# Linear attention: half of relu(k) and a 32-bit copy of v on GpSimd, with re-ordered queues

## The chip, the cores and the metric

The kernel runs on one core of a Trainium2 chip. The metric is the device time of one execution in microseconds (us), the median of several runs. Engines: TensorE (PE, and PEld for its weight loads), VectorE (DVE), ScalarE (ACT), GpSimd (POOL), and SyncE (SP, which issues all DMA transfers here). Ratios below are the mean time of one kernel's fast runs over the mean time of the fast runs of the kernel before from the same rounds, so they are not quite the ratios of the medians that are quoted. "Before" was measured anew in every set of rounds: 200.88, 200.08, 200.99 and 200.26 us. e1 to e4, e5 to e8, and the second e5 with e9 to e11 ran on three different chips, so across these groups the ratios compare better than the medians.

## The reference

32 heads, 2048 positions, 128 features, bf16:

```python
phi_q = jnp.where(q > 0, q + 1, jnp.exp(q)) + 1e-6
phi_k = jnp.where(k > 0, k + 1, jnp.exp(k)) + 1e-6
kv = jnp.einsum("bhsd,bhse->bhde", phi_k, v)
z = jnp.einsum("bhsd->bhd", phi_k)
num = jnp.einsum("bhqd,bhde->bhqe", phi_q, kv)
den = jnp.einsum("bhqd,bhd->bhq", phi_q, z)[..., None] + 1e-6
return num / den
```

The kernels use phi(x) = (min(exp(x), 1) + 1e-6) + relu(x). The two terms are separate stationary operands of TensorE, which adds them up.

## The kernel before

A head has 16 tiles of 128 positions. Its steps, with the names used below:

| name | engine | work |
|---|---|---|
| ek, eq | ScalarE | exp(k), exp(q) of the whole head |
| em, emq | VectorE | min with 1 and add 1e-6, in SBUF |
| rk | VectorE | relu(k), SBUF to SBUF |
| rqa, rqb | ScalarE, VectorE | relu of the transposed q, read from PSUM, half each; in every fourth head ScalarE does all |
| v1 | GpSimd | copies v next to a column of ones |
| T | TensorE | 16 transposes of q |
| kv, then kvs | TensorE, then ScalarE | 32 matmuls; copy of the 128x129 sum |
| n | TensorE | numerator and denominator: 12 tiles (nA, later n.0), 4 tiles (nC, later n.1) |
| r, f | VectorE | reciprocal and multiply, read from PSUM |

```python
    NI = 8      # buffers for k, q, v
    NO = 6      # output buffers
    LAG = 2     # a store is issued two heads behind
# ...
        def emrk(h):
            s = h % 2
            add("DVE", f"em{h}", lambda e: e.tensor_scalar(
                em_sb[:, s], em_sb[:, s], 1.0, EPS, op0=ALU.min, op1=ALU.add), [f"ek{h}"])
            add("DVE", f"rk{h}", lambda e: e.tensor_scalar(
                rk_sb[:, s], k_sb[:, h % NI], 0.0, None, op0=ALU.max), [f"ldk{h}"] + ([f"kv{h - 2}"] if h >= 2 else []))
# ...
        def v1(h):
            dep = [f"ldv{h}"]
            if h >= 2:
                dep += [f"kv{h - 2}"]
            if h >= 3:
                dep += [f"nA{h - 3}"]        # the gate: not needed for the data
            add("POOL", f"v1{h}", lambda e: e.tensor_scalar(
                v1_sb[:, h % 2, :, 0:D], v_sb[:, h % NI].rearrange("p (j d) -> p j d", d=D), 1.0, 0.0,
                op0=ALU.mult, op1=ALU.add), dep)
# ... the order of the instructions, head i
            eq(i)
            rqa(i)
            kvs(i + 1)
            ek(i + 2)
            f(i - 1, "A")
            rqb(i)
            emq(i)
            f(i - 1, "C")
            emrk(i + 2)
            T(i + 1)
            nA(i)
            nC(i)
            kv(i + 2)
```

Of the kernel before, what the change touches and what calls it, by code (L numbers as in the profile page):

```python
# [8 lines left out]
ENGINES = ("PE", "DVE", "ACT", "POOL", "SP")  # L9

# [5 lines left out]
class Program:  # L16



    def __init__(self, sem):  # L20
        self.sem = sem
        self.ops = {e: [] for e in ENGINES}
        self.where = {}
        self.count = {}
        self.sems = {}

    def add(self, eng, key, fn, deps=(), dma=None, inc=True):

        name = dma if dma is not None else eng
        if dma is not None or inc:  # L30
            self.count[name] = self.count.get(name, 0) + (16 if dma is not None else 1)
        if key is not None:
            assert key not in self.where, key
            assert dma is not None or inc
            self.where[key] = (name, self.count[name], eng, len(self.ops[eng]))
        self.ops[eng].append((fn, tuple(deps), name, (16 if dma is not None else 1) if (dma is not None or inc) else 0))
# [47 lines left out]
def _eps_pieces():  # L84

    import struct

    def bf(x):
        u = struct.unpack("<I", struct.pack("<f", x))[0]
        u = (u + 0x7FFF + ((u >> 16) & 1)) & 0xFFFF0000  # L90
        return struct.unpack("<f", struct.pack("<I", u))[0]

    a = bf(EPS / 128)
    b = bf(EPS - 126 * a)
    return a, b, bf(EPS - 126 * a - b)


def bass_standalone__linear_attn_elu__prompt_kernel(nc: bass.Bass, q: bass.AP, k: bass.AP, v: bass.AP, out: bass.AP):
    B, H, S, D = q.shape
    assert D == P and S == 16 * P  # L100
    NT = S // P
    NH = B * H
    bf16, fp32 = mybir.dt.bfloat16, mybir.dt.float32
    N = NT * D
    NC = D + 1
    NI = 8
    NO = 6
    LAG = 2
# [4 lines left out]
    with ExitStack() as es:  # L113
# [11 lines left out]
        k_sb, q_sb, v_sb = sb([P, NI, N]), sb([P, NI, N]), sb([P, NI, N])  # L125
        em_sb, rk_sb = sb([P, 2, N]), sb([P, 2, N])
        v1_sb = sb([P, 2, NT, NC])
        emq_sb, rq_sb = sb([P, 2, N]), sb([P, 2, N])
        kvs_sb = sb([P, 2, NC])
        rden_sb = sb([P, 2, NT], fp32)  # L130
        o_sb = sb([P, NO, NT, D])
        ident, ones, epsr, one1 = sb([P, P]), sb([P, P]), sb([P, 3]), sb([P, 1])
        xT = alloc(nc.psum_tensor, [P, N], bf16)
# [3 lines left out]
        CO = 4 * 512  # L137

        def slot(t):
            if t < 12:  # L140
                return 512 * (t // 3) + NC * (t % 3)
            return CO + 512 * ((t - 12) // 2) + NC * ((t - 12) % 2)

        pr = Program(sem)
        add = pr.add


# [9 lines left out]
        for s in range(2):  # L157
            add("DVE", f"v1ones{s}", lambda g, s=s: g.memset(v1_sb[:, s, :, D:NC], 1.0))


        def load(name, dst, src, h, freed):
            dep = [f"{f}{h - NI}" for f in freed] if h >= NI else []
            add("SP", f"ld{name}{h}", lambda e: e.dma_start(
                dst[:, h % NI].rearrange("p (j d) -> p j d", d=D), rows(src, h)), dep, dma=f"{name}{h % NI}")

        def loads(h):
            load("k", k_sb, kf, h, ["ek", "rk"])
            load("q", q_sb, qf, h, ["T"])
            load("v", v_sb, vf, h, ["v1"])

        def store(h):
            s = h % NO
            if h < NH - 1:
                add("SP", f"st{h}", lambda e: e.dma_start(rows(of, h), o_sb[:, s]), [f"fA{h}", f"fC{h}"], dma=f"o{s}")
            else:
                add("SP", None, lambda e: e.dma_start(rows(of, h)[:, 0:12, :], o_sb[:, s, 0:12]), [f"fA{h}"], dma=f"o{s}")
                add("SP", f"st{h}", lambda e: e.dma_start(rows(of, h)[:, 12:NT, :], o_sb[:, s, 12:NT]), [f"fC{h}"],
                    dma=f"o{s}")

        for h in range(min(NI, NH)):  # L180
            loads(h)
        for h in range(NH + LAG):
            if h + NI < NH:
                loads(h + NI)
            if h >= LAG:
                store(h - LAG)


        def ek(h):
            add("ACT", f"ek{h}", lambda e: e.activation(em_sb[:, h % 2], k_sb[:, h % NI], ACT.Exp),  # L190
                [f"ldk{h}"] + ([f"kv{h - 2}"] if h >= 2 else []))

        def eq(h):
            add("ACT", f"eq{h}", lambda e: e.activation(emq_sb[:, h % 2], xT[:, :], ACT.Exp),  # L194
                [f"T{h}"] + ([f"nC{h - 2}"] if h >= 2 else []))

        def split(h):
            return h % 4 != 3

        def rqa(h):  # L200
            n = N // 2 if split(h) else N
            add("ACT", f"rqa{h}", lambda e: e.activation(rq_sb[:, h % 2, 0:n], xT[:, 0:n], ACT.Relu),  # L202
                [f"T{h}"] + ([f"nC{h - 2}"] if h >= 2 else []))

        def rqb(h):
            if split(h):
                add("DVE", f"rqb{h}", lambda e: e.tensor_scalar(  # L207
                    rq_sb[:, h % 2, N // 2:], xT[:, N // 2:], 0.0, None, op0=ALU.max),
                    [f"eq{h}"] + ([f"nC{h - 2}"] if h >= 2 else []))

        def rqs(h):
            return [f"rqa{h}"] + ([f"rqb{h}"] if split(h) else [])

        def kvs(h):
            add("ACT", f"kvs{h}", lambda e: e.activation(kvs_sb[:, h % 2], kv_ps, ACT.Copy),  # L215
                [f"kv{h}"] + ([f"nC{h - 2}"] if h >= 2 else []))

        def emrk(h):
            s = h % 2
            add("DVE", f"em{h}", lambda e: e.tensor_scalar(  # L220
                em_sb[:, s], em_sb[:, s], 1.0, EPS, op0=ALU.min, op1=ALU.add), [f"ek{h}"])
            add("DVE", f"rk{h}", lambda e: e.tensor_scalar(  # L222
                rk_sb[:, s], k_sb[:, h % NI], 0.0, None, op0=ALU.max), [f"ldk{h}"] + ([f"kv{h - 2}"] if h >= 2 else []))

        def emq(h):
            s = h % 2
            add("DVE", f"emq{h}", lambda e: e.tensor_scalar(  # L227
                emq_sb[:, s], emq_sb[:, s], 1.0, EPS, op0=ALU.min, op1=ALU.add), [f"eq{h}"])

        def v1(h):  # L230
            dep = [f"ldv{h}"]
            if h >= 2:
                dep += [f"kv{h - 2}"]
            if h >= 3:
                dep += [f"nA{h - 3}"]
            add("POOL", f"v1{h}", lambda e: e.tensor_scalar(  # L236
                v1_sb[:, h % 2, :, 0:D], v_sb[:, h % NI].rearrange("p (j d) -> p j d", d=D), 1.0, 0.0,
                op0=ALU.mult, op1=ALU.add), dep)

        def T(h):  # L240
            def f(e):
                for j in range(NT):
                    ins = e.transpose(xT[:, j * P:(j + 1) * P], q_sb[:, h % NI, j * D:(j + 1) * D], ident[:])  # L243
                return ins
            add("PE", f"T{h}", f, [f"ldq{h}", "ident"] + (([f"eq{h - 1}"] + rqs(h - 1)) if h else []))

        def kv(h):
            def f(e):
                for j in range(NT):
                    for part, src in ((0, em_sb), (1, rk_sb)):  # L250
                        ins = e.matmul(kv_ps, lhsT=src[:, h % 2, j * D:(j + 1) * D], rhs=v1_sb[:, h % 2, j, :],  # L251
                                       start=(j + part == 0), stop=(j == NT - 1 and part == 1))
                return ins
            add("PE", f"kv{h}", f, [f"em{h}", f"rk{h}", f"v1{h}", "v1ones0", "v1ones1"] + ([f"kvs{h - 1}"] if h else [])
                + ([f"fC{h - 3}"] if h >= 3 else []))

        def num(h, tiles, bank, n, e):
            s = h % 2
            e.matmul(_ap(o_ps[:, :], slot(tiles[0]) + D, [[NC, n]]), lhsT=ones[:], rhs=epsr[:, 0:n], start=True, stop=False,  # L259
                     skip_group_check=True)  # L260
            for t in tiles:
                o = o_ps[:, slot(t):slot(t) + NC]
                e.matmul(o, lhsT=emq_sb[:, s, t * P:(t + 1) * P], rhs=kvs_sb[:, s, :], start=False, stop=False,  # L263
                         skip_group_check=True)
                ins = e.matmul(o, lhsT=rq_sb[:, s, t * P:(t + 1) * P], rhs=kvs_sb[:, s, :], start=False, stop=True,  # L265
                               skip_group_check=True)
            return ins

        def nA(h):
            def f(e):  # L270
                for b in range(4):
                    ins = num(h, range(3 * b, 3 * b + 3), b, 3, e)
                return ins
# [3 lines left out]
        def nC(h):  # L277
            def f(e):
                num(h, (12, 13), 4, 2, e)
                return num(h, (14, 15), 5, 2, e)  # L280
# [126 lines left out]
```

## Time and profile before

200.87 us (199.35 to 201.48, three runs). The page of the profiled execution gives busy time and share of each engine (first lines), the DMA engines' busy tenths and GB/s in 40 slices of the span, and the chain that ended last by engine:

```profile
span 197.3 us, 6384 instructions
PE 170.6 (86%) x2842; PEld 160.5 (81%) x2842; DVE 161.6 (82%) x254; ACT 160.0 (81%) x129; POOL 68.4 (35%) x38
...
DMA  6999999999999999999999999999999622222133
GB/s 228 346 418 411 412 404 407 410 404 416 416 411 422 412 416 419 411 420 414 414 420 413 419 418 414 419 414 417 416 415 394 246 116 110 106 106 105 61 130 137
...
ACT 37%; PE 33%; DVE 22%; DMA 3%; issue 2%; POOL 1%; SPq 0%
```

No engine is full: three stand at 81 to 86%, and the chain alternates between them. DMA is at its rate (394 to 422 GB/s a slice) from 10 to about 155 us. The view of waits shows whom the engines waited for (total us, times, longest):

```profile
POOL la L236 <- PE la L265: 97.5, 29, 3.5
DVE la L220 <- ACT la L190: 27.4, 32, 7.1
ACT la L215 <- PE la L251: 23.0, 25, 4.0
...
POOL la L236 <- DMA la<-in_v_dram: 11.5, 3, 6.5
```

ScalarE's copy of kv (L215) waits for kv, and VectorE's em (L220) for exp(k). That is a chain through three engines: kv, kvs, ek, em, rk, next kv. GpSimd's wait is its gate and costs next to nothing: TensorE waited 0.2 us in all for the copy (same view). The timeline of one head on VectorE and GpSimd (start us, duration us, engine, line, operation; in brackets the idle time before):

```profile
103.40 0.69 DVE L220 TENSOR_SCALAR la<-la 128x2048 bf16<-128x2048 bf16 x1 [0.88 <-ACT la L190]
104.01 0.69 DVE L222 TENSOR_SCALAR la<-la 128x2048 bf16<-128x2048 bf16 x1
104.06 2.39 POOL L236 TENSOR_SCALAR la<-la 128x2048 bf16<-128x2048 bf16 x1 [3.13 <-PE la L265]
104.61 0.23 DVE L293 RECIPROCAL la<-la 128x12 f32<-128x12 f32 x1
...
104.87 1.76 DVE L299 TENSOR_TENSOR la<-la 128x1536 bf16<-128x1536 f32 x1
106.54 0.68 DVE L207 TENSOR_SCALAR la<-la 128x1024 bf16<-128x1024 bf16 x1
...
108.92 0.69 DVE L220 TENSOR_SCALAR la<-la 128x2048 bf16<-128x2048 bf16 x1 [0.28 <-ACT la L190]
```

The pitch of an operation is the distance from its start to the next start; it is shorter than the duration, because the next operation starts before the end (em ends at 104.09, rk starts at 104.01). From em to em a head takes 5.52 us. GpSimd's copy, 1.90 us where it is undisturbed, shows 2.39 us here: it started while VectorE's rk (L222) was under way.

### The profile page before, as it was taken

What the parts mean: (1) busy time and instruction counts of PE and PEld (TensorE: products, weight loads), DVE (VectorE), ACT (ScalarE), POOL (GpSimd) and SP (SyncE); (2) the same over time, 40 slices, a digit from 0 to 9 for tenths busy, and PEclk for the clock granted to TensorE, in tenths of its full rate; (3) what the DMA queues carried; (4) which work ended last, traced back from release to release, by engine and by line L of the source; (5) the groups of instructions that cost most, each with busy time, mean ns of one, the idle gap of its engine ahead of it and who ended that gap; (6) DMA issues with size and microseconds to landing.
All of it is one profiled execution on the core that took longest, in us unless ns stands there. A gap on an engine that the chain in (4) does not pass through costs nothing.

```text
span 197.3 us, 6384 instructions
## 1 busy us (share of the span) xinstructions
PE 170.6 (86%) x2842; PEld 160.5 (81%) x2842; DVE 161.6 (82%) x254; ACT 160.0 (81%) x129; POOL 68.4 (35%) x38
## 2 busy tenths in 40 slices
PE   6948999988898899988898889988898889988850
PEld 6938889888897889888897889888897889988850
DVE  0213899899989999899989999899989999899774
ACT  4563789988898889988898889988898889998530
POOL 1333343322344444332344444432344444431000
PEclk9997999999999999999999999999999999999985
DMA  6999999999999999999999999999999622222133
GB/s 228 346 418 411 412 404 407 410 404 416 416 411 422 412 416 419 411 420 414 414 420 413 419 418 414 419 414 417 416 415 394 246 116 110 106 106 105 61 130 137
DMA packets 18603, 67.52 MB, mean 342 GB/s; under 512 B 2064, under 2 KB 2192, under 8 KB 18576
## 3 DMA queue, kind: packets, MB, share of 16 engines
q1 hardware_dynamic: 18576, 67.12, 84.4%
q8 instruction: 22, 0.36, 0.7%
q14 instruction: 5, 0.04, 0.1%
HBM read 50.33 MB, written 16.78 MB: 340 GB/s over the span
## 4 chain that ended last, share of the span: by engine, by line
ACT 37%; PE 33%; DVE 22%; DMA 3%; issue 2%; POOL 1%; SPq 0%
ACT la L190 21%; PE la L251 18%; DVE la L299 9%; ACT la L202 6%; ACT la L194 6%; DVE la L220 6%; PE la L243 5%; PE la L263 5%; PE la L265 5%; DVE la L222 4%; DMA la<-in_v_dram 3%; ACT la L215 3%; DVE la L207 2%; DVE la L293 1%; POOL la L236 1%
## 5 line engine op out<-in xcount | busy, mean ns | idle before, releaser
L236 POOL TENSOR_SCALAR la<-la 128x2048 bf16<-128x2048 bf16 x32 | 67.7, 2116 | 109.1 <-PE la L265 97.5
L299 DVE TENSOR_TENSOR la<-la 128x1536 bf16<-128x1536 f32 x64 | 78.4, 1224 | 2.2
L251 PE MATMUL la<-la 128*128 128x129 bf16 x1024 | 65.3, 222 | 5.7 <-DVE la L222 5.4
L251 PEld LDWEIGHTS la<-la 128*128 128x128 bf16 x1024 | 59.7, 98 | 10.2 <-DVE la L222 7.1
L265 PE MATMUL la<-la 128*128 128x129 bf16 x512 | 66.7, 221 | 0.0
L263 PE MATMUL la<-la 128*128 128x129 bf16 x512 | 66.6, 220 | 0.0
L194 ACT ACTIVATE la<-la 128x2048 bf16<-128x2048 bf16 x32 | 59.8, 1869 | 3.7 <-PE la L243 3.7
L190 ACT ACTIVATE la<-la 128x2048 bf16<-128x2048 bf16 x32 | 60.9, 1902 | 1.9 <-DMA la<-in_k_dram 1.9
L265 PEld LDWEIGHTS la<-la 128*128 128x128 bf16 x512 | 49.8, 97 | 0.0
L263 PEld LDWEIGHTS la<-la 128*128 128x128 bf16 x512 | 47.6, 98 | 0.0
L243 PE MATMUL la<-la 128*128 128x128 bf16 x512 | 35.0, 222 | 12.7 <-DVE la L207 11.5
L220 DVE TENSOR_SCALAR la<-la 128x2048 bf16<-128x2048 bf16 x32 | 22.2, 694 | 27.4 <-ACT la L190 27.4
L243 PEld LDWEIGHTS la<-la 128*128 128x128 bf16 x512 | 29.6, 99 | 18.0 <-DVE la L207 15.5
L202 ACT ACTIVATE la<-la 128x1024 bf16<-128x1024 bf16 (+1 forms) x32 | 39.6, 1238 | 0.0
L259 PE MATMUL la<-la 128*128 128x3 bf16 (+1 forms) x192 | 32.5, 169 | 2.2 <-DVE la L227 2.2
L215 ACT ACTIVATE la<-la 128x129 bf16<-128x129 f32 x32 | 9.0, 280 | 23.0 <-PE la L251 23.0
L222 DVE TENSOR_SCALAR la<-la 128x2048 bf16<-128x2048 bf16 x32 | 22.0, 687 | 0.0
L227 DVE TENSOR_SCALAR la<-la 128x2048 bf16<-128x2048 bf16 x32 | 21.8, 683 | 0.0
L259 PEld LDWEIGHTS la<-la 128*128 128x128 bf16 x192 | 19.0, 99 | 2.4 <-DVE la L227 2.4
L207 DVE TENSOR_SCALAR la<-la 128x1024 bf16<-128x1024 bf16 x24 | 16.3, 681 | 0.0
L293 DVE RECIPROCAL la<-la 128x12 f32<-128x12 f32 x64 | 12.9, 201 | 2.5 <-PE la L265 2.5
L308 PE MATMUL la<-la 128*128 128x120 bf16 x90 | 7.6, 268 | 1.5 <-POOL la L149 1.5
(13 smaller groups left out, 9.9 us busy)
## 6 DMA issues: line engine op xcount, KB each, us to landing
la<-in_k_dram SPq DMA_DIRECT2D x32, 512.0 KB, 15.0
la<-in_q_dram SPq DMA_DIRECT2D x32, 512.0 KB, 15.0
la<-in_v_dram SPq DMA_DIRECT2D x32, 512.0 KB, 15.2
out_dram<-la SPq DMA_DIRECT2D x31, 512.0 KB, 15.1
out_dram<-la SPq DMA_DIRECT2D x1, 384.0 KB, 2.3
out_dram<-la SPq DMA_DIRECT2D x1, 128.0 KB, 2.1
```

Source lines behind the costliest of these rows:

```text
L190: add("ACT", f"ek{h}", lambda e: e.activation(em_sb[:, h % 2], k_sb[:, h % NI], ACT.Exp), [f"ldk{h}"] + ([f"kv{h - 2}"] if h >= 2 else []))
L194: add("ACT", f"eq{h}", lambda e: e.activation(emq_sb[:, h % 2], xT[:, :], ACT.Exp), [f"T{h}"] + ([f"nC{h - 2}"] if h >= 2 else []))
L202: add("ACT", f"rqa{h}", lambda e: e.activation(rq_sb[:, h % 2, 0:n], xT[:, 0:n], ACT.Relu), [f"T{h}"] + ([f"nC{h - 2}"] if h >= 2 else []))
L220: add("DVE", f"em{h}", lambda e: e.tensor_scalar(em_sb[:, s], em_sb[:, s], 1.0, EPS, op0=ALU.min, op1=ALU.add), [f"ek{h}"])
L222: add("DVE", f"rk{h}", lambda e: e.tensor_scalar(rk_sb[:, s], k_sb[:, h % NI], 0.0, None, op0=ALU.max), [f"ldk{h}"] + ([f"kv{h - 2}"] if h ...
L236: add("POOL", f"v1{h}", lambda e: e.tensor_scalar(v1_sb[:, h % 2, :, 0:D], v_sb[:, h % NI].rearrange("p (j d) -> p j d", d=D), 1.0, 0.0, o ...
L243: ins = e.transpose(xT[:, j * P:(j + 1) * P], q_sb[:, h % NI, j * D:(j + 1) * D], ident[:])
L251: ins = e.matmul(kv_ps, lhsT=src[:, h % 2, j * D:(j + 1) * D], rhs=v1_sb[:, h % 2, j, :], start=(j + part == 0), stop=(j == NT - 1 and par ...
L259: e.matmul(_ap(o_ps[:, :], slot(tiles[0]) + D, [[NC, n]]), lhsT=ones[:], rhs=epsr[:, 0:n], start=True, stop=False, skip_group_check=True)
L263: e.matmul(o, lhsT=emq_sb[:, s, t * P:(t + 1) * P], rhs=kvs_sb[:, s, :], start=False, stop=False, skip_group_check=True)
L265: ins = e.matmul(o, lhsT=rq_sb[:, s, t * P:(t + 1) * P], rhs=kvs_sb[:, s, :], start=False, stop=True, skip_group_check=True)
L299: add("DVE", f"f{which}{h}", lambda e: e.tensor_tensor(out=_ap(o_sb[:, :, :, :], ob + t0 * D, [[n * D, nb], [D, n], [1, D]]), in0=_ap(o_ps ...
```

## The change

Intent: take work from VectorE, lengthen the look-ahead between the engines, and let loads go ahead of stores. The new kernel names every instruction and gives each engine an explicit list (called "annealed" below). Its core:

```diff
-    NI = 8
-    NO = 6
+NI, NO, NE, NR, NV, NQ, NK = 7, 12, 2, 2, 2, 2, 2
+RKP = (8, 8, ...)   # tiles of relu(k) on GpSimd, of 16
+NA = (8, 8, ...)    # tiles of relu(q) on ScalarE, now 8 in every head
+def gate(name, h):
+    return []
 # relu(k), lower 8 tiles
 add("DVE", f"rkd{h}.{i}", ... e.tensor_scalar(rk_sb[...a:b], k_sb[...a:b], 0.0, None, op0=ALU.max)
 # relu(k), upper 8 tiles
+add("POOL", f"rkp{h}.{i}", ... e.tensor_scalar(rk_sb[...a:b], k_sb[...a:b], BIG, 0.0, op0=ALU.min, op1=ALU.max),
+    ldk + kv{h-2} + gate("rkp", h))
 # copy of v
-add("POOL", f"v1{h}", ... e.tensor_scalar(v1_sb[..., 0:D], v_sb[...], 1.0, 0.0, op0=ALU.mult, op1=ALU.add), dep)
+add("POOL", f"v1{h}.{i}", ... e.tensor_copy(v1_sb[...].bitcast(i32), v_sb[...].bitcast(i32)),
+    ldv + kv{h-2} + gate("v1", h))
 # orders, here around the 9th head (excerpts)
+"PE":  ... n8.0 T10.0 n8.1 kv10.0 kv10.1 n9.0 T11.0 n9.1 kv11.0 kv11.1 ...
+"DVE": ... r7.0 rkd10.0 f7.0 em10.0 r7.1 rqb9 f7.1 rkd11.0 r8.0 emq9.0 f8.0 em11.0 rqb10 r8.1 f8.1 ...
+"ACT": ... ek10.0 eq9.0 kvs9 rqa9 ek11.0 eq10.0 kvs10 rqa10 ...
+"POOL": ... rkp11.0 v111.0 v112.0 rkp13.0 v113.0 rkp12.0 rkp14.0 v114.0 ...
+"SP":  ... st4.0 ldq17.0 ldv15.0 st1.0 ldq21.0 ldv17.0 ldv18.0 st2.0 st3.0 ldk18.0 ldk20.0 ...
```

(The lists are cut; "..." also stands for indices.) Transposes and exp(q) now run two heads ahead of the division. The first head is done in halves, the last head's division and store in three groups.

## The prediction

> **What bounds the kernel now.** After a prologue, every head takes 5.525 us (pitch of exp(k) in the timeline). No engine is full in it. By pitches in the timeline: VectorE needs 5.25 us in the three heads of four in which it does half of relu(q), ScalarE 4.7 (5.5 in the fourth), TensorE about 4.7 (n 1.5 + 0.5, T 0.9, kv 1.8). The chain of waits alternates ScalarE (37%), TensorE (33%), VectorE (22%): kv -> kv copy -> exp(k) -> min/add. ScalarE waits 23.0 us in all for kv (waits view). GpSimd works 2.1 us per head, gated by the division matmuls so that it falls under VectorE's PSUM work. DMA runs at 416 GB/s up to 155 us but only early loads are waited for; 67.1 MB at 416 GB/s is 161 us, a floor close by. The first division matmul starts at 19.6 us, the last head's at 189.9, 7.4 us before the end.
>
> **What changes.** (a) Half of relu(k) leaves VectorE: 0.60 us of pitch -> about 0.33. (b) relu(q) is always split: ScalarE 4.7 us in every head; VectorE loses the cheap fourth head. Its sum: 0.26+0.60+1.68+0.60+0.33+0.21+0.60+0.69 = 4.97 us. (c) GpSimd gets two operations of 1024 elements; from 1.90 us for 2048 (undisturbed, timeline) I estimate 1.0 us each if a 32-bit element costs what a 16-bit one does: 2.0 us per head, as before. (d) The orders run transposes and exp(q) two heads ahead of the division, so the chain kv -> copy -> exp(k) -> kv is no longer closed within a head. (e) Twelve output buffers let stores wait.
>
> Sums now: VectorE 4.97, ScalarE 4.7, TensorE 4.7, DMA 2.1 MB / 416 GB/s = 5.04 us per head.
>
> **The cost.** The gate on GpSimd is gone: it starts when kv ends, by my count about half a microsecond before the large PSUM division ends, and min/add of exp(k) follows that at once. The Trainium skill, "SBUF — State Buffer", section "Who interferes with whom", says a VectorE operation in a two-port mode and a GpSimd operation block each other fully. This trace shows one side: GpSimd's copy takes 2.39 us instead of 1.90 when it starts 0.05 us into VectorE's relu(k) of 0.6 us. VectorE was never the blocked side here (each form varies by under 10 ns). I expect VectorE to lose 0.2 to 0.5 us per head.
>
> Period: about 5.2 us (4.97 without collisions, 5.6 with two per head). All of it is on the path.
>
> **Ends.** Halves and orders: first division matmul near 13 to 14 us, third near 25 us (30.7 before): about 5 us saved. Last head: about 6 us instead of 7.4.
>
> Span: 25.2 + 29 x 5.2 + 6 = 182; timed runs lie 2 to 4 us above the profiled span: about 184.5 us, range 178 to 194. Faster 0.90, same 0.06, slower 0.04.
>
> **Right or wrong in the profile.** Pitch of exp(k) 5.1 to 5.3 us; VectorE busy over 90% in the middle; GpSimd's two forms near 1.0 us each, many longer; VectorE's SBUF-to-SBUF forms now with a spread of several tenths; DMA near 1.0 almost to the end and less of a tail at 106 GB/s.
>
> **What would make it wrong.** The 32-bit copy or min-max costing twice per element (kv then waits for GpSimd); VectorE blocked twice per head; a load stuck behind another in the shuffled queue, seen as waits for DMA; the lower granted clock.

## The result

185.22 us (184.55 to 186.80, four runs): ratio 0.9238, 95% interval 0.9165 to 0.9310. The output is correct. The profiled execution is the slowest of the four (186.80 us), and the one before was a fast one: in all listed runs the time lies about 1.8 us above the span, so 197.3 us stands for about 199.1 us (an estimate). The two profiles therefore show 12.3 us of the 15.7 between the medians. The page of the changed kernel, the same parts as before:

```profile
span 185.0 us, 6438 instructions
PE 165.2 (89%) x2842; PEld 159.1 (86%) x2842; DVE 164.4 (89%) x266; ACT 155.2 (84%) x131; POOL 75.4 (41%) x71
...
DMA  5999999999999999938999999799999999968994
GB/s 175 322 411 416 407 409 405 409 406 375 352 318 423 408 410 415 403 109 272 414 417 378 302 416 414 283 363 391 348 414 418 413 424 412 384 251 335 398 409 170
...
DVE 38%; DMA 26%; PE 12%; SPq 10%; issue 6%; ACT 3%; POOL 2%; DVEq 0%; POOLq 0%
```

VectorE is busy longer than before (164.4 against 161.6 us) although it was given less to do (half of relu(k) less in every head, half of relu(q) more in every fourth). DMA has holes: 109 GB/s in the slice from 79 to 83 us. A quarter of the chain is now DMA. The waits:

```profile
POOL la L324 <- DMA la<-in_v_dram: 27.5, 13, 5.5
...
ACT la L345 <- PE la L368: 11.0, 14, 1.7
...
DVE la L316 <- DMA la<-in_k_dram: 4.7, 4, 2.4
...
DVE la L313 <- ACT la L310: 3.9, 4, 1.7
...
ACT la L336 <- PE la L331: 2.7, 4, 1.3
```

The chain through three engines is open: VectorE's wait for exp(k) fell from 27.4 to 3.9 us, ScalarE's for kv from 23.0 to 2.7. In its place stand 13 waits of GpSimd for v, 4 of VectorE for k, and a new one: ScalarE's exp(q) (L345) waits 11.0 us for the division's matmuls.

One head on VectorE without any GpSimd operation inside it (timeline):

```profile
101.48 0.22 DVE L375 RECIPROCAL la<-la 128x12 f32<-128x12 f32 x1
101.62 0.63 DVE L347 TENSOR_SCALAR la<-la 128x2048 bf16<-128x2048 bf16 x1
102.17 1.74 DVE L382 TENSOR_TENSOR la<-la 128x1536 bf16<-128x1536 f32 x1
103.83 0.68 DVE L313 TENSOR_SCALAR la<-la 128x2048 bf16<-128x2048 bf16 x1
104.47 0.43 DVE L316 TENSOR_SCALAR la<-la 128x1024 bf16<-128x1024 bf16 x1
104.82 0.18 DVE L375 RECIPROCAL la<-la 128x4 f32<-128x4 f32 x1
104.91 0.66 DVE L354 TENSOR_SCALAR la<-la 128x1024 bf16<-128x1024 bf16 x1
105.49 0.68 DVE L382 TENSOR_TENSOR la<-la 128x512 bf16<-128x512 f32 x1
106.08 0.22 DVE L375 RECIPROCAL la<-la 128x12 f32<-128x12 f32 x1
```

That is 4.60 us of VectorE work. Where GpSimd is at work it looks different (timeline, with GpSimd):

```profile
49.16 1.03 POOL L324 COPY la<-la 128x1024 int32<-128x1024 int32 x1
...
49.64 1.10 DVE L347 TENSOR_SCALAR la<-la 128x2048 bf16<-128x2048 bf16 x1
...
54.19 1.03 POOL L324 COPY la<-la 128x1024 int32<-128x1024 int32 x1
54.53 1.24 DVE L347 TENSOR_SCALAR la<-la 128x2048 bf16<-128x2048 bf16 x1
```

The same emq (L347) took 0.63 us in the quiet head; it takes 1.10 and 1.24 us when it starts 0.48 and 0.34 us into GpSimd's copy. Both times it ends 0.55 us after the copy does (50.19 and 55.22), so the earlier it starts, the longer it stands. rqb (L354), which reads PSUM, does not spread: it lies between 0.652 and 0.692 us in the whole trace. This is the side of the exclusion that the trace before could not show, and it agrees with the Trainium skill, "SBUF — State Buffer", section "Who interferes with whom", by which the later of the two waits until the earlier is through.

The holes in DMA come from the issuing queue (timeline of SP, with one line of TensorE, the transposes of head 14):

```profile
69.12 0.47 SPq L298 DMA_DIRECT2D la<-in_v_dram  x1
69.63 0.44 SPq L390 DMA_DIRECT2D out_dram<-la  x1
...
79.86 1.06 PE L342 MATMUL la<-la 128*128 128x128 bf16 x16
...
80.95 0.33 SPq L298 DMA_DIRECT2D la<-in_q_dram  x1
81.32 1.29 SPq L298 DMA_DIRECT2D la<-in_v_dram  x2
```

For 11 us nothing was issued. The next entry was the q load of head 21, whose buffer is freed by the transposes of head 14 (through at 80.92). Loads and stores behind it stood, whether they were ready or not.

Where the 12.3 us between the two profiled spans lie, from the first division matmul of a head:

| part | before | after | gain |
|---|---|---|---|
| start to head 2 | 30.84 | 26.73 | 4.1 |
| head 2 to head 31 | 159.02 (29 x 5.48) | 149.94 (29 x 5.17) | 9.1 |
| head 31 to end | 7.4 | 8.3 | -0.9 |

### The profile page after: what moved, and what is told of

It is laid out like the page before. It is cut to its first block, busy times and chain, and to the rows that moved or that the text cites. A ratio compares the mean times of both kernels' runs of the same rounds, so it can differ in the third digit from the quotient of the medians.

```text
span 185.0 us, 6438 instructions
## 1 busy us (share of the span) xinstructions
PE 165.2 (89%) x2842; PEld 159.1 (86%) x2842; DVE 164.4 (89%) x266; ACT 155.2 (84%) x131; POOL 75.4 (41%) x71
## 4 chain that ended last, share of the span: by engine, by line
DVE 38%; DMA 26%; PE 12%; SPq 10%; issue 6%; ACT 3%; POOL 2%; DVEq 0%; POOLq 0%
DVE la L382 18%; DMA la<-in_k_dram 11%; DMA out_dram<-la 9%; SPq L298 8%; DMA la<-in_v_dram 6%; DVE la L347 6%; DVE la L354 5%; DVE la L316 4%; DVE la L313 4%; PE la L366 4%; PE la L368 3%; PE la L342 3%; ACT la L345 2%; DVE la L375 2%; PE la L331 2%
## 5 line engine op out<-in xcount | busy, mean ns | idle before, releaser
L382 DVE TENSOR_TENSOR la<-la 128x1536 bf16<-128x1536 f32 (+2 forms) x65 | 77.5, 1196 | 1.2 <-DMA out_dram<-la 0.6
L345 ACT ACTIVATE la<-la 128x2048 bf16<-128x2048 bf16 (+1 forms) x33 | 60.2, 1825 | 12.3 <-PE la L368 11.0
L368 PE MATMUL la<-la 128*128 128x129 bf16 x512 | 69.6, 222 | 0.0
L366 PE MATMUL la<-la 128*128 128x129 bf16 x512 | 69.5, 221 | 0.0
L331 PE MATMUL la<-la 128*128 128x129 bf16 x1024 | 64.5, 219 | 2.1 <-POOL la L324 2.0
L310 ACT ACTIVATE la<-la 128x2048 bf16<-128x2048 bf16 (+1 forms) x33 | 61.3, 1860 | 3.0 <-DMA la<-in_k_dram 2.9
L320 POOL TENSOR_SCALAR la<-la 128x1024 bf16<-128x1024 bf16 x32 | 40.4, 1264 | 46.0 <-PE la L331 38.1
L324 POOL COPY la<-la 128x1024 int32<-128x1024 int32 (+1 forms) x33 | 35.2, 1070 | 44.3 <-DMA la<-in_v_dram 27.5
L342 PE MATMUL la<-la 128*128 128x128 bf16 x512 | 34.1, 219 | 5.3 <-DVE la L354 5.3
L351 ACT ACTIVATE la<-la 128x1024 bf16<-128x1024 bf16 x32 | 32.6, 1018 | 0.0
L313 DVE TENSOR_SCALAR la<-la 128x2048 bf16<-128x2048 bf16 (+1 forms) x33 | 24.5, 743 | 3.9 <-ACT la L310 3.9
L347 DVE TENSOR_SCALAR la<-la 128x2048 bf16<-128x2048 bf16 (+1 forms) x33 | 25.2, 765 | 1.8 <-ACT la L345 1.8
L316 DVE TENSOR_SCALAR la<-la 128x1024 bf16<-128x1024 bf16 x32 | 19.7, 615 | 5.5 <-DMA la<-in_k_dram 4.7
L354 DVE TENSOR_SCALAR la<-la 128x1024 bf16<-128x1024 bf16 x32 | 21.3, 667 | 0.5 <-ACT la L345 0.4
L375 DVE RECIPROCAL la<-la 128x12 f32<-128x12 f32 (+2 forms) x65 | 12.7, 197 | 3.7 <-PE la L368 3.0
```

The lines of the kernel that those rows point to most:

```text
L310: add("ACT", f"ek{h}.{i}", lambda e, a=a, b=b: e.activation(em_sb[:, h % NE, a:b], k_sb[:, h % NI, a:b], ACT.Exp), [f"ldk{h}.{i}"] + freed ...
L320: add("POOL", f"rkp{h}.{i}", lambda e, a=a, b=b: e.tensor_scalar(rk_sb[:, h % NR, a:b], k_sb[:, h % NI, a:b], BIG, 0.0, op0=ALU.min, op1=A ...
L324: add("POOL", f"v1{h}.{i}", lambda e, a=a, b=b: e.tensor_copy(v1_sb[:, h % NV, a:b, 0:D].bitcast(i32), v_sb[:, h % NI, a:b].bitcast(i32)), ...
L331: ins = e.matmul(kv_ps, lhsT=src[:, j], rhs=v1_sb[:, h % NV, j, 0:NC], start=(j + part == 0), stop=(j == NT - 1 and part == 1))
L342: ins = e.transpose(xT[:, j], q_sb[:, h % NI, j], ident[:])
L345: add("ACT", f"eq{h}.{i}", lambda e, a=a, b=b: e.activation(emq_sb[:, h % NQ, a:b], xT[:, a:b], ACT.Exp), [f"T{h}.{i}"] + freed(NQ, h, ("n ...
```

## The experiments

Theory A is the prediction's: VectorE, with its collisions with GpSimd, sets the pitch. Rival B: late loads from the order of the DMA queue set it, and collisions hide behind them. Twelve runs of eleven kernels were made on these and on what came up; all were correct. "Pitch" is the mean distance between the copies of kv of heads 3 and 29 on ScalarE (before 5.52, after 5.25).

### e1: relu(k) back on VectorE

```diff
-RKP = (8, 8, ...)
+RKP = (0,) * 32      # all of rk is rkd on VectorE; rkp dropped from GpSimd's list
```

> The changed kernel with all of relu(k) back on VectorE; GpSimd only copies v as 32-bit words. Theory A (VectorE, with its collisions with GpSimd, sets the pitch): VectorE gains 0.27 us of work a head, from 4.60 (the pitch of an undisturbed head at 101.5 to 106.1 us) to 4.87, and loses the collisions with one of GpSimd's two operations (about half of the 0.4 us that a head takes over 4.60 where no load is late). Net 0 to +0.15 us a head: 185 to 190 us. If moving relu(k) pays in full, it is 8 us slower: 193. Theory B (late loads set the pitch): no change, 185 within 1%, because the loads wait for the same events.

185.05 us, ratio 0.9256 (0.9160 to 0.9352); pitch 5.23. No difference from the changed kernel: the headline of the change pays nothing in its own setting. Both theories allowed for this, A by an even trade of work for collisions.

### e2: only the DMA queue mended

```diff
+    first = ORDER["SP"].split()
+    out = first[:first.index("ldk9.0")] + ["ldv6.0", "ldq6.0"]      # the first loads as they were
+    for h in range(7, 32):
+        out += [f"ldv{h}.0", f"ldk{h}.0", f"ldq{h}.0"]
+        if h >= 16:
+            out.append(f"st{h - 16}.0")
+    # the remaining stores follow in order (shortened: names put in as numbers)
```

> The changed kernel with only the order of the DMA queue replaced from the 20th load on: v, k, q of one head after another, a store seven heads behind. Theory A (VectorE with collisions sets the pitch): at most 1% faster, pitch stays near 5.25. Theory B (the queue stands behind loads that are asked for too early, 11 to 13 us at a time at 69.6, 105.7 and 147.9 us, and the next k and v come late): the waits of VectorE and GpSimd for k and v go (4.7 and 27.5 us now), DMA has no slice under 300 GB/s up to 140 us, the pitch falls from 5.25 to the 5.03 of the stretch from 37 to 58 us: 178 to 180 us.

180.86 us, ratio 0.9064 (0.8998 to 0.9129); pitch 5.05. The page's DMA line has no hole left:

```profile
GB/s 185 284 413 416 409 411 405 411 405 411 403 409 406 404 410 409 415 416 414 420 411 416 420 414 420 411 417 417 414 419 415 414 420 414 415 334 178 121 155 199
```

GpSimd's waits for v fell from 27.5 to 10.4 us. So B holds for 2.3% of the time by the medians (180.86 against 185.22), 1.9% by the ratios, a little less than expected. Heads of 5.5 to 5.8 us remain between heads of 4.72.

### e3 and e4: GpSimd tied to VectorE

```diff
 def gate(name, h):
-    return []
+    if h < 4:
+        return []
+    return [f"rkd{h}.0"] if name == "rkp" else [f"emq{h - 2}.0"]
```

with GpSimd's list made regular (rkp4 v14 rkp5 v15 ...). e3 does this alone, e4 with e2's queue.

> The changed kernel with GpSimd's two operations tied to VectorE: relu(k) starts after VectorE's own half of the same head, the copy of v after VectorE's min/add of exp(q) two heads back, so that both fall under VectorE's reads of PSUM; GpSimd's order made regular. Theory A: the VectorE forms of SBUF to SBUF lose their spread (maxima 1.26 to 1.52 us now, medians 0.43 to 0.68), GpSimd's two forms stay near 1.04, pitch where loads are in time 4.7 to 4.8 instead of 5.03; time 178 to 183 us if late loads leave it. Theory B: collisions go but the time stays within 1% of 185, the gained time turns into waits for loads.

> Both of the last two. If collisions and late loads are two separate costs, the pitch comes to 4.7 to 4.85 us (VectorE 4.60, TensorE and ScalarE 4.7, DMA 5.04 averaged but with stores put off): 170 to 175 us. If one hides the other, no better than the better of the two alone.

e3: 184.16 us, ratio 0.9213 (0.9139 to 0.9287), no different from the changed kernel. e4: 182.96 us, ratio 0.9176 (0.9116 to 0.9235), 1% slower than e2, though their intervals just overlap. The expectation for e4 was missed by 8 us. Its heads are 4.72 us in places, but some are 6.3 and 6.8: VectorE's annealed list has rkd at irregular places, and a GpSimd operation tied to it comes late; TensorE now waits 4.2 us for GpSimd's copy. A gate alone in an order made without it was no test of what collisions cost in the changed kernel's own order.

### e5: the headline in the old order

The kernel before, with relu(k) of 8 tiles on GpSimd (min-max, waits for its k and for kv two heads back) and the 32-bit copy; the gate on the copy stays:

```diff
-                rk_sb[:, s], k_sb[:, h % NI], 0.0, None, op0=ALU.max)
+                rk_sb[:, s, 0:N // 2], k_sb[:, h % NI, 0:N // 2], 0.0, None, op0=ALU.max)
+            add("POOL", f"rkp{h}", lambda e: e.tensor_scalar(
+                rk_sb[:, h % 2, N // 2:], k_sb[:, h % NI, N // 2:], BIG, 0.0, op0=ALU.min, op1=ALU.max),
+                [f"ldk{h}"] + ([f"kv{h - 2}"] if h >= 2 else []))
```

(Cut: the copy itself, and the rows of v1, which are two bytes longer, as in the changed kernel.)

> The kernel before with only the announced part of the change: GpSimd does relu(k) of 8 tiles by min and max and copies v as 32-bit words; orders, buffers and gate as before. Theory A (taking 0.27 us a head from VectorE is what paid): the chain kv, copy, exp(k), min/add, relu(k) gets shorter in the heads where relu(k) ends it: 195 to 197 us. Theory C, formed after the first four runs (the gain came from the orders, which open that chain; the split alone pays nothing): 199 to 202 us, pitch still about 5.5.

> The same kernel as e5_before_split again, whose profiled execution fell into a state with TensorE at about a fifth of its pace (895 us; the three timed ones were 206.7 to 208.4). Expected: 206 to 209 us, and a profile that shows why the announced part alone is slower. Theory D (the ungated relu(k) on GpSimd blocks VectorE): SBUF-to-SBUF forms of VectorE with maxima above 1 us, pitch 5.7 to 5.8. Rival E (kv waits for GpSimd's relu(k) itself): waits of TensorE for GpSimd of some tenths of a us a head, VectorE's forms without spread.

The first time 208.36 us (ratio 1.0356), with one execution of 897 us, which the profile happened to catch; the second time 208.13 us, ratio 1.0363 (1.0269 to 1.0457), pitch 5.82. The announced part alone makes the kernel 3.6% slower; both theories of the first expectation (195 to 197, 199 to 202) were wrong. The timeline of the second profile shows why:

```profile
100.37 1.04 POOL L238 TENSOR_SCALAR la<-la 128x1024 bf16<-128x1024 bf16 x1 [1.33 <-PE la L255]
100.52 1.44 DVE L229 TENSOR_SCALAR la<-la 128x2048 bf16<-128x2048 bf16 x1
```

The instructions of emq by line (duration ns min/median/max), in the kernel before and in e5:

```profile
L227 DVE TENSOR_SCALAR la<-la x32: 682/683/684, 16.0 to 189.1; 128x2048 bf16<-128x2048 bf16 x32
...
L229 DVE TENSOR_SCALAR la<-la x32: 675/1294/1512, 15.7 to 197.7; 128x2048 bf16<-128x2048 bf16 x32
```

GpSimd's relu(k) starts when kv ends and keeps its 1.04 us; emq, 0.15 us later, stands until it is through (101.41) and ends at 101.96. It happens in most heads: the median went from 0.683 to 1.294 us. VectorE is busy for 176.2 us against 161.6. TensorE has no wait for GpSimd beyond the first microseconds, so rival E falls and D holds. A version with this operation gated was not run in the old order.

### e6: does relu(k) on GpSimd pay with loads in time?

e2 with e1's edit.

> The mended DMA queue (180.9 us) with all of relu(k) back on VectorE. If relu(k) on GpSimd pays once loads are in time: VectorE 4.87 against 4.60 us a head shows, 183 to 188 us. If it only trades VectorE's work for VectorE's waits[...]: 180 to 182 us, within 1% of the mended queue alone.

178.21 us, ratio 0.8876 (0.8816 to 0.8936); pitch 4.99. It is 1.5% faster than e2, and the intervals do not touch; both expected ranges were too high. By the copies of kv in the two profiles, e6 is ahead by 0.9 us at head 0 (its first transposes start that much earlier; why was not followed up), by 3.0 at head 4 and by 3.7 at head 31. Between heads 0 and 4, e2 shows an emq of 1.52 us and halves of relu(k) of 1.25 to 1.29. So once the loads are in time, relu(k) on GpSimd costs more in collisions than it takes off VectorE in the first heads, and in the later ones the trade is about even.

### e7 and e8: one order for every head, without and with the gate

e2's queue, and from head 4 on one order for every head; e8 adds the gate from head 7 on. Cut here: one swap on TensorE, which puts T15 before n13.1 as in the other heads.

```diff
+    for i in range(4, 29):
+        dve += [f"r{i}.0", f"emq{i + 1}.0", f"f{i}.0", f"em{i + 3}.0", f"rkd{i + 3}.0", f"r{i}.1", f"rqb{i + 2}", f"f{i}.1"]
+    for h in range(6, NH):
+        pool += [f"v1{h}.0", f"rkp{h}.0"]
 # e8 only
 def gate(name, h):
-    return []
+    if h < 7:
+        return []
+    return [f"rkd{h}.0"] if name == "rkp" else [f"emq{h - 2}.0"]
```

> The mended queue with the annealed orders of VectorE and GpSimd replaced from the fifth head on by one order that repeats for every head (relu(k) always three heads ahead of the division), no gate. If the irregular orders cause the heads of 5.5 to 6.8 us beside those of 4.72 (ScalarE's sum), the pitch becomes even, 4.75 to 4.9: 173 to 177 us. If those heads come from collisions with GpSimd alone, the pitch stays near 5.05 and the time near 181.

> The same with GpSimd's two operations tied to VectorE's progress so that they fall under its reads of PSUM. If collisions still cost in the regular order, the VectorE forms of SBUF to SBUF lose their maxima above 1 us and the pitch reaches ScalarE's 4.72: 171 to 174 us, 1 to 2% below the ungated one. If the ungated regular order already avoids them, the two are within 1%.

e7: 187.83 us, ratio 0.9360 (0.9307 to 0.9413), heads of 5.71 and 4.72 us in turn. Neither of the two expectations (173 to 177, near 181) held: regular order without a gate is slower than the annealed one. e8: 175.73 us, ratio 0.8744 (0.8667 to 0.8821), a steady 4.72 us between the copies of kv of heads 7 to 29. Its time missed the expected 171 to 174 by 2 us, and the gain over e7 was far more than the expected 1 to 2%. The timelines of a head, e7 first:

```profile
105.43 1.22 POOL L358 COPY la<-la 128x1024 int32<-128x1024 int32 x1 [2.48 <-PE la L365]
105.68 1.25 DVE L350 TENSOR_SCALAR la<-la 128x1024 bf16<-128x1024 bf16 x1
106.62 1.21 POOL L354 TENSOR_SCALAR la<-la 128x1024 bf16<-128x1024 bf16 x1
```

then e8:

```profile
104.77 0.42 DVE L352 TENSOR_SCALAR la<-la 128x1024 bf16<-128x1024 bf16 x1
...
105.27 1.04 POOL L356 TENSOR_SCALAR la<-la 128x1024 bf16<-128x1024 bf16 x1 [1.58 <-DVE la L352]
...
107.23 1.75 DVE L418 TENSOR_TENSOR la<-la 128x1536 bf16<-128x1536 f32 x1
107.38 1.04 POOL L360 COPY la<-la 128x1024 int32<-128x1024 int32 x1 [1.07 <-DVE la L383]
108.89 0.69 DVE L349 TENSOR_SCALAR la<-la 128x2048 bf16<-128x2048 bf16 x1
```

In e7 GpSimd starts when kv ends, as in the changed kernel, and in every second head VectorE's half of relu(k) takes 1.25 us instead of 0.42. In e8 both GpSimd operations lie under VectorE's reads of PSUM, and each keeps its 1.04 us. From 35 us on VectorE's forms there hardly spread: em 0.68 to 0.69 us, emq 0.62 to 0.68, rkd 0.42 but for one of 0.85. The gate is worth 6.4% in this order (175.73 against 187.83). e8 is the best kernel: 5.1% under the changed one, 12.6% under the one before. Its pitch is ScalarE's own sum, 1.81 (ek) + 1.84 (eq) + 0.17 (kvs) + 0.90 (rqa) = 4.72 by pitches in the timeline, which shows no wait of ScalarE in these heads.

### e9: relu(k) on VectorE in the gated kernel

e8 with e1's edit.

> The regular gated kernel (175.7 us) with relu(k) wholly on VectorE. Without collisions on either side VectorE needs 4.87 us a head against ScalarE's 4.72: pitch 4.87 to 4.95, 178 to 182 us, so that relu(k) on GpSimd pays 1.5 to 3% once it is gated. If it pays nothing even so: 175 to 176.5.

177.02 us, ratio 0.8814 (0.8736 to 0.8892). Gated, relu(k) on GpSimd seems to pay 0.8%, less than expected, but the intervals of e8 and e9 overlap and the time lies between the two expected ranges: neither a gain nor its size is settled.

### e10: the copy of v in 16-bit elements

```diff
-                    v1_sb[:, h % NV, a:b, 0:D].bitcast(i32), v_sb[:, h % NI, a:b].bitcast(i32)),
+                    v1_sb[:, h % NV, a:b, 0:D], v_sb[:, h % NI, a:b]),
```

> The regular gated kernel with v copied as 2048 16-bit elements instead of 1024 words of 32 bits. GpSimd's copy takes 1.9 us instead of 1.04, longer than the 1.66 us of VectorE's large PSUM division it lies under, so min/add of exp(k) waits 0.2 to 0.35 us a head: VectorE 4.8 to 4.95, pitch 4.8 to 4.95 against 4.72, 177 to 183 us. If 16-bit elements are copied as fast as 32-bit words, nothing changes.

182.47 us, ratio of the fast runs 0.9002 (0.8878 to 0.9126); two of the four runs count as slow, and the mean of the other two is 180.8. The copy takes 1.889 us for 2048 elements of 16 bits against 1.04 us for the same bytes as 1024 words. em, which follows the large division, went from 0.68 to 0.92 us and the steady head from 4.72 to 4.79 us. That is about 1.4 us over the kernel. Most of the rest is one head of 9.4 us at the start (5.6 in e8), where GpSimd is not yet gated: there em takes 2.23 us, begun 0.21 us into the longer copy. So the 32-bit copy pays in this kernel, most of it where operations collide; without a gate throughout it was not tried apart.

### e11: stores two heads behind instead of seven

```diff
-LAG = 9
+LAG = 4
```

> The regular gated kernel with each store two heads behind instead of seven (the twelve output buffers not used to put stores off). DMA then carries 2.1 MB a head at 416 GB/s, 5.04 us, from the start: loads fall behind, waits for k and v in the second half, pitch there up to 5.04: 178 to 183 us. If the first loads' lead lasts to the end: 175 to 177.

176.62 us, ratio 0.8797 (0.8727 to 0.8868): 0.5% over e8, inside the intervals, with the same heads of 4.72 us up to head 28. In the gated kernel, putting stores off was not needed.

## Why the prediction was right

The time was foretold within 0.4% (184.5 against 185.22 us), but the closeness is partly luck: errors cancel in the sum, and one of its risks came true. In the profile the sum reads 26.7 + 29 x 5.17 + 8.3 = 185.0 us, not 25.2 + 29 x 5.2 + 6 = 182. The profiled execution was 1.6 us above the median, and timed runs lie 1.8 us above their own span, not 2.5; this makes up the difference.

- **Collisions of VectorE with GpSimd: right.** VectorE's SBUF-to-SBUF forms spread from 0.36 to 1.26 us (relu) and to 1.52 us (emq) while rqb, which reads PSUM, does not. Predicted 0.2 to 0.5 us a head. From 38 to 58 us, where loads were in time and VectorE was busy 19.99 of 20.1 us, a head takes 5.03 us against 4.60 in the quiet one: 0.43 us. By pitches about 0.36 of it stands in the SBUF-to-SBUF forms (an estimate); the rest lies mostly behind the small reciprocal. This window is the evidence for the changed kernel's own order, since the gate of e3 was no clean test there; e5, and e7 against e8, show in two other orders that collisions are on the path.
- **VectorE's sum of 4.97 us: too high by 0.37.** The prediction took the pitches of the old order. There a multiply follows its reciprocal at once and starts 0.26 us after it (104.61 to 104.87); in the new order an independent operation mostly stands between and starts after 0.14 us. The two reciprocals of a head make up 0.24 of the 0.37. With 4.60 us VectorE is not even the longest engine by its own work: ScalarE needs 4.72, as e8 shows. The prediction's floor without collisions should have been 4.72, not 4.97.
- **Period 5.2 us: right in size (5.17), by a different sum.** The prediction has 4.97 of work and about 0.23 of collisions. The trace has 4.60 of work and 0.43 over it where loads are in time, and the remaining 0.14 goes with the late loads (an estimate: 5.17 less 5.03). The prediction named a load stuck in the shuffled queue only as a risk and put it at nothing; e2 puts it at 4.4 us by the medians, 3.5 by the ratios. Accordingly "DMA near 1.0 almost to the end" was wrong where the queue stood.
- **"Half of relu(k) leaves VectorE" as a gain: wrong.** e1 puts its worth in the changed kernel at nothing, e6 at minus 1.5% with loads in time (most of it in the first heads), e5, with the 32-bit copy, at minus 3.6% in the old order. VectorE was busier after than before. The prediction's own terms say as much: 0.27 us a head saved, 0.2 to 0.5 lost. Only with GpSimd placed (e8 against e9) may it pay, by 0.8%.
- **(d), the open chain: right,** by the two waits that fell from 27.4 and 23.0 us to 3.9 and 2.7. e1, which has all of the change but relu(k) on GpSimd, gains as much, so the gain lies in the rest: orders, buffers, the first head in halves, the 32-bit copy and relu(q) split in every head. That the orders carry most of it is argued from the waits, not shown. How much belongs to relu(q) was not run apart; from ScalarE's pitches (0.8 us in 8 heads of 32) it is at most about 6 us, an estimate.
- **Ends.** The first division matmul came at 12.65 us (13 to 14 predicted). The third head began at 26.7 us instead of 25: 4.1 us saved, not 5, with VectorE forms of 1.25 and 1.52 us from collisions at 17 to 19 us. The last head took 8.3 us, not 6. The trace shows a part of why: from 176.6 to 180.4 us the granted clock was 0.55, and the last head's matmuls took 0.32 us instead of 0.22 and 3.7 us in all, against 2.3 in the kernel before (clock 0.73 from 189.8 to 192.3 us). Why the clock fell there is open.

## What to carry to other kernels

Before moving work to an engine that can block a busy one, ask when it will start, not only how long it takes. Here the same two GpSimd operations cost 6% when they started at the end of a matmul group (e7), against a tie to a point after which VectorE reads PSUM for 1.4 us or more (e8). The tie has to fit the order: in the annealed one (e4) it gained nothing, and TensorE waited 4.2 us for the copy. In SyncE's queue an entry that waited for its buffer held back all that followed (11 us here), so entries belong in the order in which their buffers come free. When a prediction is right, check its terms one by one: here one was 0.37 us a head too high, and two together about as much too low.

## What the Trainium skill lacked or had wrong

- "GPSIMD Engine Reference", section "Elementwise — side-by-side cycle accounting", gives about 1.03 cycles an element for a body of at most two operations, and the slope here agrees: in e10 copies of 2048 and 1024 bf16 elements take 1.889 and 1.038 us, so an element takes 0.83 ns, 1.0 cycle at the 1.2 GHz that the page states. That section gives no time by the width of the element. Here the width made no difference: 1024 bf16 elements 1.038 us, 1024 int32 words 1.04 us. The page "VectorE: DVE Perf Modes" has this trick (a bf16 copy reinterpreted as INT32) for VectorE only.
- "SBUF — State Buffer", section "Who interferes with whom", is right about the exclusion in both directions (GpSimd's copy 1.90 to 2.39 us, VectorE's emq 0.68 to 1.44 us). That section lacks the remedy that worked: tie the GpSimd operation by a semaphore to a VectorE operation that is followed by PSUM reads (187.83 to 175.73 us).
- "VectorE: DVE Perf Modes", section "The DRAIN you can't avoid", measures that semaphores between copies cost nothing. It gives no such figure for an operation that needs the result just before it. In the changed kernel's trace a multiply right behind its large reciprocal mostly started 0.25 us after that one's start (7 times), an independent operation 0.14 us (21 times).
- No page read says what an entry that waits in SyncE's DMA queue does to those behind it: 11 us without an issue, 109 GB/s instead of 410.
- "TensorE: Matmul & The Clock Gate", section "Seeing it yourself", reports the clock gate stuck at a quarter for over 50 us. One execution here (of e5) ran for 895 us with TensorE busy for 887 us and matmuls of 0.63 to 0.72 us on the mean by group instead of 0.22, while the granted clock in the records read 1.0. It was seen once in all the runs, and its cause is open.
